# Layer two's attention steps in another order, and three pairs of banks in the last nested product: one Trainium2 core

## The chip, the core and the metric

The kernel runs on one core of a Trainium2 chip, in one launch. The core has five engines with a queue of instructions each, worked off strictly in order: TensorE (PE in the profile, with its weight loads as PEld), VectorE (DVE), ScalarE (ACT), GpSimd (POOL) and SyncE (SP, which here only issues DMA transfers). An engine goes on until an instruction needs something that another engine or a transfer hasn't finished; then everything behind it in that queue waits too. Matmuls write to PSUM, which has eight banks of 128 x 512 numbers. The metric is the device time of one execution in microseconds.

## What is computed

Two layers of linear attention and two of a gated mixer alternate on a sequence of 2048 rows of 512 numbers, all in fp32:

```python
def _A_ref(x, wqkv, wo):                    # H = 32, Dh = 16
    q, k, v = split_heads(x @ wqkv)
    phi = lambda t: jnp.where(t > 0, t + 1, jnp.exp(t)) + 1e-6
    pq, pk = phi(q), phi(k)
    kv = jnp.einsum("bhsd,bhse->bhde", pk, v)
    z = jnp.einsum("bhsd->bhd", pk)
    num = jnp.einsum("bhqd,bhde->bhqe", pq, kv)
    den = jnp.einsum("bhqd,bhd->bhq", pq, z)[..., None] + 1e-6
    return merge_heads(num / den) @ wo

def _B_ref(x, w_in, w_sp, b_sp, w_out):     # Fh = 896
    z = _gelu(jnp.einsum("bsd,df->bsf", x, w_in))
    z1, z2 = z[..., :Fh], _layernorm(z[..., Fh:], axis=-1)
    g = jnp.einsum("ts,bsf->btf", w_sp, z2) + b_sp[None, :, None]
    return jnp.einsum("bsf,fd->bsd", z1 * g, w_out)

x = A_x
x = x + _A_ref(_layernorm(x, axis=-1), A_wqkv, A_wo)
x = x + _B_ref(_layernorm(x, axis=-1), B_w_in, B_w_sp, B_b_sp, B_w_out)
x = x + _A_ref(_layernorm(x, axis=-1), A_wqkv, A_wo)
x = x + _B_ref(_layernorm(x, axis=-1), B_w_in, B_w_sp, B_b_sp, B_w_out)
```

## The kernel before

**Precision.** Each fp32 operand of a matmul is cut into a high part, which ScalarE rounds (`high`, line 132), and a low part, the rest, which VectorE subtracts (`low`, line 135). A product is then three matmuls (`mm3`, lines 146 to 148): high by high, high by low, low by high.

**Tiles.** Rows are worked on in 16 tiles of 128. In SBUF there are slots of several sizes: 22 pages ("pg", 128 x 512), 6 quads ("qd", four pages each), 4 larger ones ("bg") and the 16 tags z0 to z15. A slot is taken from the front of a list and put back at its end, and the next holder's first write waits for the last one's reads. The order of all instructions is the order in which the Python code issues them; nothing is rescheduled behind it.

**The attention loop (class `P1`, method `run`).** One step s works on several row tiles at once. `T_high(s)` transposes tile s on VectorE (line 327, its source is a copy that was written to DRAM turned, loaded by `turn.load`) and rounds it on ScalarE; `T_low(s)` subtracts. `K(s-1)` and `Q(s-1)` are 12 matmuls each, and `Gmm(s-2)` another 12, onto four banks which hold G over the whole loop. `K_phi` and `Q_phi` apply phi: two activations (lines 414, 415) and a sum on VectorE that reads the PSUM bank (line 416). `xsplit(s-1)` cuts the row tile itself, `K_split(s-1)` cuts phi(K) (lines 427 and 428) and lets GpSimd add it to a running sum (`zacc`, line 433). The Q of the last six tiles (`DEFER`) is put off into the steps behind the loop, so steps 11 to 16 have K and G only.

In layer two the same loop carries other work. `own.staged()` makes one part per step of the kept sums of the mixer's weights for the product N4: VectorE takes the low part of the sum before, ScalarE the high part of the next, VectorE adds or subtracts for the one after (lines 1244 to 1254), and SP stores parts and fetches pieces. From step 5 on, one piece per step of the weights wo and win2 is cut into high and low (`side`), and the next is fetched. Step 1 normalises the last row tile (`norm`), step 2 sends it to DRAM (`send`), step 15 loads wv into the quads in which the kept sums' pages lay until then.

In the order of issue, a step of layer two before the change is: loads of x and of the turned tile; T_high; K; T_low; K_phi; Q; xsplit; K_split; staged; Q_phi; Gmm; the side piece; the next side fetch.

**The nested product N4 (class `P4`, `nested_mm`).** The mixer's product w_sp by z2 is cut into block products; N1, N2 and N4 are themselves cut into seven (P1 to P7, Strassen in Winograd's form), each of two steps of 12 matmuls. Some of the seven add onto the banks of one before them. In N4, the last in layer two, VectorE adds or subtracts each of the seven, as soon as it is done, from the output (line 1468), and the banks go on being added to:

```python
NEST = {p: ("P1", "P2", "P6", "P5", "P7", "P3", "P4") for p in ("N1", "N2")}
NEST["N4"] = "P1", "P6", "P2", "P5", "P7", "P4", "P3"
```

with X (two banks) for P1, P6, P7, P4, and Y (two) for P2, and anew for P5 and P3. Step g issues, in this order: `prepare(g + 2, g + 3)` (high and low of weights, lines 1361 and 1370, and of the other operand), the matmuls, the sums if a product is done, `fetch(g + 4)`, gates on GpSimd (line 1548) and a load for the next gate. P1, P2 and P4 load 512 KB of raw weights per step on SP's queue (line 1314) and split them. P5, P6, P7 and P3 load 1024 KB per step on GpSimd's queue (line 1307): the kept sums, already split.

The functions that the change touches, with what calls them:

Of the kernel before, what the change touches and what calls it, by code (L numbers as in the profile page):

```python
# [11 lines left out]
F32R = mybir.dt.float32r  # L12
# [3 lines left out]
P = 128  # L16
# [10 lines left out]
DEFER = 6  # L27
# [57 lines left out]
def mixer_kernel(ctx: ExitStack, tc: tile.TileContext, x_in, wqkv, wo_d, win1_d, win2_d, wsp_d, bsp_d, wout_d,  # L85
# [246 lines left out]
    class P1:  # L332
# [91 lines left out]
        def K_split(self, i):  # L424
            r = self.r.pop(i)
            h, l = pages.get(PAGE, F32R), pages.get(PAGE, F32R)
            nc.scalar.activation(h, r, AF.Copy, bias=PHI_EPS)
            nc.vector.scalar_tensor_tensor(l, r, PHI_EPS, h.bitcast(F32), op0=OP.add, op1=OP.subtract)
            self.pk[i] = (h, l)
            if i == 0:  # L430
                self.zacc = r
            else:
                nc.gpsimd.tensor_tensor(r, self.zacc, r, op=OP.add)
                pages.put(self.zacc)
                self.zacc = r
# [22 lines left out]
        def xsplit(self, i):  # L458
            h, l = pages.get(PAGE, F32R), pages.get(PAGE, F32R)
            x = self.x.pop(i)  # L460
            if self.turn.turned(i):
                split(feats(h, False), feats(l, False), feats(x, True))
            else:
                split(h, l, x)
            pages.put(x)
            self.xhl[i] = (h, l)
# [80 lines left out]
        def run(self):  # L547
            side = deque()
            for w in (self.wo, self.win2):
                side.extend([w] * len(w.pieces))  # L550
            ND = NT - DEFER
            own = inner["N4"] if self.L == 1 else None
            if own is not None:
                spare = quads.get([P, 2, 2, 512]), quads.get([P, 2, 2, 512])
                own.home = Views(pages, *spare)
            else:
                self.wv = quads.get([P, 4, 512])
            each = 2 if own is None else 1
            for s in range(1, NT + 2):
                if s == 2 and own is not None:  # L560
                    self.send(NT - 1)
                self.loadx(s + 3 if own is None else s + 1)
# [22 lines left out]
                if own is not None and s <= NT:  # L585
                    own.staged()
                    if s == 1:
                        self.norm(NT - 1)
                    if s == NT - 1:
                        own.home.close()  # L590
                        own.home = pages
                        quads.put(*spare)
                        self.wv = quads.get([P, 4, 512])
# [9 lines left out]
                for c in (range(4) if s == NT - 1 else ()) if own is not None else range(s - 1, min(s, 4)):  # L603
                    nc.sync.dma_start(self.wv[:, c, :], wqkv[c * P:(c + 1) * P, 1024:1536])
                if s > 4:
                    for _ in range(min(len(side), 1 if s < 6 else each)):
                        side.popleft().piece()
                if s >= 4:
                    for w in list(side)[:1 if s < 5 else each]:
                        w.fetch()  # L610

# [655 lines left out]
    class P4:  # L1267
# [9 lines left out]
        NEST["N4"] = "P1", "P6", "P2", "P5", "P7", "P4", "P3"  # L1277
# [158 lines left out]
        def nested_mm(self, g):  # L1436
# [25 lines left out]
            if p == "N4":  # L1462
                for n, out in {"P1": ((1, self.X),), "P6": ((2, self.X),), "P2": ((1, self.Y),), "P5": ((4, self.Y),),
                               "P7": ((4, self.X),), "P3": ((2, self.Y),), "P4": ((3, self.X),)}[name]:
                    for i in range(2):
                        f = i if n % 2 else 2 + i
                        u = self.unit(n // 3, f)
                        (V.tensor_add if f == 3 else V.tensor_sub)(u, u, out[i])  # L1468
                if name in ("P2", "P3"):
                    banks.put(*self.Y)  # L1470
                elif name == "P4":
                    banks.put(*self.X)
                if name == "P3":
                    self.ready.extend((n, f, False) for n in range(2) for f in range(NF))
                return
            for i in range(2):
# [7 lines left out]
                elif name == "P2":  # L1484
                    V.tensor_add(u[1], u[1], self.Y[i])
# [8 lines left out]
                if name in ("P2", "P3"):  # L1494
                    banks.put(self.Y[i])
                elif name == "P4":
                    banks.put(self.X[i])
# [340 lines left out]
```

## Time and profile before

| | |
|---|---|
| three runs, median (lowest to highest) | 1377.22 us (1373.12 to 1379.17) |
| the profiled execution | 1374.07 us, of which the span is 1372.4 us |
| granted TensorE clock over the span | 0.999 |
| HBM traffic | 223 GB/s over the span |
| layer two's attention loop, steps 1 to 17 | from 691 to about 815 us of the span |
| N4, 14 steps | from 1251 to 1292 us of the span |

How to read what is quoted. A row of groups or of the timeline gives start and length in us (or a sum and a mean), the engine, the line of the code, the operation, and out<-in by the tiles' names; behind it in brackets stands how long the engine stood idle before it, and what ended that. The list of waits says which engine waited at which line, for which engine and line; then the sum in us, how often, and the longest. A row of the table of windows gives a stretch of the span, its length, the busy time of TensorE, its weight loads, VectorE, ScalarE and GpSimd with the number of instructions in brackets, the granted TensorE clock, the busy share of the DMA engines and GB/s. Matmuls overlap at their ends, so busy times of TensorE say little of its pace; starts and counts say more. A row of DMA issues gives the queue, how many, their size and the median us from issue to landing. The chain of waits is followed back from the last instruction of the span.

### The profile page before, as it was taken

How to read it: one execution, taken by the hardware profiler on the slowest of the kernel's cores; microseconds unless marked ns; L12 is line 12 of the kernel's file. 1: busy time of each engine (PE TensorE's matmuls, PEld its weight loads, DVE VectorE, ACT ScalarE, POOL GpSimd, SP SyncE). 2: the span in 40 equal slices, each digit the busy share in tenths (PEclk: the TensorE clock that was granted, in tenths of full speed). 3: DMA queues.
4: the chain of work that ended last, by engine and by line, in shares of the span. 5: the costliest groups of instructions: out<-in, count | busy, mean ns of one | idle time of the engine just before them, and what ended most of it. 6: DMA issues, size and time to landing. Idle time of an engine off the chain costs nothing. (4 is left out here: it accounts for less than half of the span.)

```text
span 1372.4 us, 18248 instructions
## 1 busy us (share of the span) xinstructions
PE 1359.8 (99%) x6105; PEld 1135.9 (83%) x6105; DVE 1024.9 (75%) x1541; ACT 627.2 (46%) x1004; POOL 468.9 (34%) x539
## 2 busy tenths in 40 slices
PE   9999999999999999999999999999999999999998
PEld 7888888888888888888888778888888888888787
DVE  6775888764747789988778868876767798878542
ACT  6775543444442442533456555544465534533310
POOL 3333475433334137427411233542230011313250
PEclk9999999999999999999999999999999999999999
DMA  5542477877778988888976533665568798568552
GB/s 171 177 131 62 121 239 252 265 256 269 249 258 288 312 275 277 272 324 286 319 215 187 174 108 115 207 207 192 193 207 281 223 339 316 198 199 298 211 184 90
DMA packets 182622, 306.95 MB, mean 224 GB/s; under 512 B 15488, under 2 KB 67584, under 8 KB 178432
## 3 DMA queue, kind: packets, MB, share of 16 engines
q1 hardware_dynamic: 174320, 265.81, 59.4%
q0 software_dynamic: 6336, 36.70, 7.4%
q10 hardware_dynamic: 1872, 3.28, 0.7%
q8 instruction: 48, 0.79, 0.3%
q14 instruction: 46, 0.38, 0.1%
HBM read 208.47 MB, written 97.26 MB: 223 GB/s over the span
## 5 line engine op out<-in xcount | busy, mean ns | idle before, releaser
L1526 PE MATMUL bank<-qd,pg 128*128 128x512 f32 x544 | 211.6, 389 | 0.0
L1527 PE MATMUL bank<-qd,pg 128*128 128x512 f32 x544 | 211.6, 389 | 0.0
L1528 PE MATMUL bank<-qd,pg 128*128 128x512 f32 x544 | 211.6, 389 | 0.0
L1370 DVE TENSOR_TENSOR qd<-qd,qd 128x1024 fp32r<-128x1024 f32 x104 | 147.2, 1416 | 68.2 <-ACT qd L1361 67.9
L1361 ACT ACTIVATE qd<-qd 128x1024 fp32r<-128x1024 f32 x104 | 110.1, 1058 | 125.0 <-DVE qd L1370 48.6
L132 ACT ACTIVATE pg<-pg 128x512 fp32r<-128x512 f32 (+1 forms) x154 | 94.9, 620 | 152.8 <-DVE pg L327 60.8
L148 PE MATMUL bank<-qd,pg 128*128 128x512 f32 x380 | 149.7, 394 | 0.2 <-DVE pg L135 0.2
L1117 POOL TENSOR_TENSOR pg<-pg,pg 128x512 f32<-128x512 f32 x64 | 92.7, 1449 | 138.6 <-DMA pg<-in_wsp_dram 84.4
L265 POOL TENSOR_SCALAR rs<-mv 128x1 f32<-128x1 f32 x95 | 46.9, 493 | 262.6 <-DVE mv L263 253.7
L276 ACT ACTIVATE pg<-pg,nb,rs 128x512 f32<-128x512 f32 x63 | 51.2, 813 | 170.6 <-POOL nb L270 170.3
L1548 POOL TENSOR_TENSOR bg<-bg,pg 128x512 f32<-128x512 f32 x56 | 90.8, 1631 | 110.4 <-DMA pg<-z 93.1
L135 DVE TENSOR_TENSOR pg<-pg,pg 128x512 fp32r<-128x512 f32 (+1 forms) x151 | 110.5, 733 | 18.7 <-ACT pg L132 11.2
L1527 PEld LDWEIGHTS bank<-qd,pg 128*128 128x128 f32 x544 | 102.1, 188 | 21.4
L1526 PEld LDWEIGHTS bank<-qd,pg 128*128 128x128 f32 x544 | 102.1, 188 | 21.2
L1528 PEld LDWEIGHTS bank<-qd,pg 128*128 128x128 f32 x544 | 102.1, 188 | 21.0
L146 PE MATMUL bank<-qd,pg 128*128 128x512 f32 x284 | 110.6, 390 | 0.0
L147 PE MATMUL bank<-qd,pg 128*128 128x512 f32 x284 | 110.6, 389 | 0.0
L327 DVE STREAM_TRANSPOSE pg<-pg 128x512 f32<-128x512 f32 x79 | 85.4, 1081 | 13.2 <-DMA z<-pg 4.9
L146 PE MATMUL bank<-bg,qd 128*128 128x448 f32 x256 | 94.1, 367 | 0.0
L147 PE MATMUL bank<-bg,qd 128*128 128x448 f32 x256 | 93.6, 366 | 0.0
L148 PE MATMUL bank<-bg,qd 128*128 128x448 f32 x256 | 93.5, 365 | 0.0
L1452 PE MATMUL bank<-qd,pg 128*128 128x512 f32 x224 | 87.3, 390 | 2.7 <-DVE bg L1468 2.6
(214 smaller groups left out, 3189.4 us busy)
## 6 DMA issues: line engine op xcount, KB each, us to landing
qd<-s SPq DMA_DIRECT2D x64, 512.0 KB, 4.0
qd<-n POOLq DMA_DIRECT2D x32, 1024.0 KB, 8.2
pg<-in_wsp_dram SPq DMA_DIRECT2D x103, 256.0 KB, 4.7
qd<-in_wsp_dram SPq DMA_DIRECT2D x40, 512.0 KB, 4.3
n<-pg SPq DMA_DIRECT2D x70, 256.0 KB, 4.4
s<-pg SPq DMA_DIRECT2D x64, 256.0 KB, 4.4
pg<-z SPq DMA_DIRECT2D x56, 256.0 KB, 4.2
x<-pg SPq DMA_DIRECT2D x48, 256.0 KB, 3.0
```

The costliest lines, as they stand in the source:

```text
L132: nc.scalar.activation(h, src, AF.Copy)
L135: nc.vector.tensor_sub(l, src, h.bitcast(F32))
L146: nc.tensor.matmul(out, ah, bh, start=start, stop=False)
L147: nc.tensor.matmul(out, ah, bl, start=False, stop=False)
L148: nc.tensor.matmul(out, al, bh, start=False, stop=stop)
L1117: nc.gpsimd.tensor_tensor(t, a, b, op=OP.add)
L1361: nc.scalar.activation(wh, r, AF.Copy)
L1370: nc.vector.tensor_sub(wl, r, wh.bitcast(F32))
L1526: m(out, h[:, o], w[:, 0, j, :], start=start, stop=False, skip_group_check=True)
L1527: m(out, h[:, o], w[:, 1, j, :], start=False, stop=False, skip_group_check=True)
L1528: m(out, l[:, o], w[:, 0, j, :], start=False, stop=stop, skip_group_check=True)
L1548: nc.gpsimd.tensor_tensor(u, u, z1, op=OP.mult)
```

## The change

`run` is parted into `first` (layer one) and `second` (layer two). `first` issues what `run` issued for layer one. `second` issues, per step: loads of the turned tile and of x (step 2's `send` behind them); **x_high**; T_high; K; **x_low**; T_low; **staged**; K_phi; Q; **the side piece's high**; K_high; **the side piece's low**; K_low; Q_phi; Gmm; the next side fetch; and in step 15 the four loads of wv as the last. `xsplit` and `K_split` are cut in two for that.

In N4 the seven products come in the order P1, P5, P6, P2, P7, P3, P4. P2 gets a pair of banks of its own, Z (in N1 and N2 too); Y is for P5 and P3, X for P1, P6, P7 and P4. The gates of the first two chunks of rows become ready behind P4 and no more behind P3, both being the last.

```diff
         def K_split(self, i):
+            self.K_high(i)
+            self.K_low(i)
+
+        def K_high(self, i):
+            self.pk[i] = h, l = pages.get(PAGE, F32R), pages.get(PAGE, F32R)
+            nc.scalar.activation(h, self.r[i], AF.Copy, bias=PHI_EPS)
+
+        def K_low(self, i):
             r = self.r.pop(i)
-            h, l = pages.get(PAGE, F32R), pages.get(PAGE, F32R)
-            nc.scalar.activation(h, r, AF.Copy, bias=PHI_EPS)
+            h, l = self.pk[i]
             nc.vector.scalar_tensor_tensor(l, r, PHI_EPS, h.bitcast(F32), op0=OP.add, op1=OP.subtract)
-            self.pk[i] = (h, l)
...
         def xsplit(self, i):
-            h, l = pages.get(PAGE, F32R), pages.get(PAGE, F32R)
+            self.x_high(i)
+            self.x_low(i)
+
+        def x_high(self, i):
+            self.xhl[i] = h, l = pages.get(PAGE, F32R), pages.get(PAGE, F32R)
+            t = self.turn.turned(i)
+            high(feats(h, False) if t else h, feats(self.x[i], True) if t else self.x[i])
+
+        def x_low(self, i):
+            h, l = self.xhl[i]
             x = self.x.pop(i)
             if self.turn.turned(i):
-                split(feats(h, False), feats(l, False), feats(x, True))
+                low(feats(l, False), feats(x, True), feats(h, False))
             else:
-                split(h, l, x)
+                low(l, x, h)
             pages.put(x)
...
+        def second(self, side):
+            ND = NT - DEFER
+            own = inner["N4"]
+            spare = quads.get([P, 2, 2, 512]), quads.get([P, 2, 2, 512])
+            own.home = Views(pages, *spare)
+            for s in range(1, NT + 2):
+                self.turn.load(s + 1)
+                self.loadx(s + 1)
+                if s == 2:
+                    self.send(NT - 1)
+                if s <= NT:
+                    self.x_high(s - 1)
+                if 2 <= s < NT:
+                    self.T_high(s)
+                if s == 1:
+                    self.K(0)
+                    self.K(1)
+                elif 2 < s <= NT:
+                    self.K(s - 1)
+                if s <= NT:
+                    self.x_low(s - 1)
+                if 2 <= s < NT:
+                    self.T_low(s)
+                if s <= NT:
+                    own.staged()
+                    self.K_phi(s - 1)
+                if s <= ND:
+                    self.Q(s - 1)
+                if s == NT + 1:
+                    self.late()
+                if s <= NT:
+                    lows = deque()
+                    if s > 4 and side:
+                        side.popleft().piece(lows=lows)
+                    self.K_high(s - 1)
+                    for l, src, h, r in lows:
+                        low(l, src, h)
+                        pages.put(r)
+                    self.K_low(s - 1)
+                if s == 1:
+                    self.norm(NT - 1)
+                if s <= ND:
+                    self.Q_phi(s - 1)
+                if s >= 2:
+                    self.Gmm(s - 2)
+                if s == NT + 1:
+                    self.late_phi()
+                if s >= 4 and side:
+                    side[0].fetch()
+                if s == NT - 1:
+                    own.home.close()
+                    own.home = pages
+                    quads.put(*spare)
+                    self.wv = quads.get([P, 4, 512])
+                    for c in range(4):
+                        nc.sync.dma_start(self.wv[:, c, :], wqkv[c * P:(c + 1) * P, 1024:1536])
...
-        NEST["N4"] = "P1", "P6", "P2", "P5", "P7", "P4", "P3"
+        NEST["N4"] = "P1", "P5", "P6", "P2", "P7", "P3", "P4"
...
                 if name == "P1":
                     self.X = [banks.get(PAGE) for _ in range(2)]
-                elif name in ("P2", "P5"):
+                elif name == "P2":
+                    self.Z = [banks.get(PAGE) for _ in range(2)]
+                elif name == "P5":
                     self.Y = [banks.get(PAGE) for _ in range(2)]
-            out = self.Y if name in ("P2", "P5", "P3") else self.X
+            out = self.Z if name == "P2" else self.Y if name in ("P5", "P3") else self.X
...
             if p == "N4":
-                for n, out in {"P1": ((1, self.X),), "P6": ((2, self.X),), "P2": ((1, self.Y),), "P5": ((4, self.Y),),
-                               "P7": ((4, self.X),), "P3": ((2, self.Y),), "P4": ((3, self.X),)}[name]:
-                    for i in range(2):
-                        f = i if n % 2 else 2 + i
-                        u = self.unit(n // 3, f)
-                        (V.tensor_add if f == 3 else V.tensor_sub)(u, u, out[i])
-                if name in ("P2", "P3"):
-                    banks.put(*self.Y)
-                elif name == "P4":
-                    banks.put(*self.X)
-                if name == "P3":
+                n = {"P1": 1, "P6": 2, "P2": 1, "P5": 4, "P7": 4, "P3": 2, "P4": 3}[name]
+                for i in range(2):
+                    f = i if n % 2 else 2 + i
+                    u = self.unit(n // 3, f)
+                    (V.tensor_add if f == 3 else V.tensor_sub)(u, u, out[i])
+                if name in ("P2", "P3", "P4"):
+                    banks.put(*out)
+                if name == "P4":
                     self.ready.extend((n, f, False) for n in range(2) for f in range(NF))
```

More of the change, by code (lines that the diff above doesn't have):

```diff
@@ L550, in run, with first @@
                 side.extend([w] * len(w.pieces))
-            ND = NT - DEFER
[L552 to L558, printed above, removed]
+            if self.L == 0:
+                self.first(side)
+            else:
+                self.second(side)
+        def first(self, side):
+            ND = NT - DEFER
+            self.wv = quads.get([P, 4, 512])
             for s in range(1, NT + 2):
-                if s == 2 and own is not None:
-                    self.send(NT - 1)
-                self.loadx(s + 3 if own is None else s + 1)
+                self.loadx(s + 3)
                 self.turn.load(s + 1)
@@ L584, in run @@
                     self.K_split(s - 1)
[L585 to L593, printed above, removed]
                 if s + 1 < NT and s + 1 in self.turn.by_pe:
@@ L602, in run @@
                     self.late_phi()
-                for c in (range(4) if s == NT - 1 else ()) if own is not None else range(s - 1, min(s, 4)):
+                if s <= 4:
+                    c = s - 1
                     nc.sync.dma_start(self.wv[:, c, :], wqkv[c * P:(c + 1) * P, 1024:1536])
-                if s > 4:
-                    for _ in range(min(len(side), 1 if s < 6 else each)):
+                else:
+                    for _ in range(min(len(side), 1 if s < 6 else 2)):
                         side.popleft().piece()
@@ L1484, in nested_mm @@
                 elif name == "P2":
-                    V.tensor_add(u[1], u[1], self.Y[i])
+                    V.tensor_add(u[1], u[1], out[i])
                 elif name == "P5":
@@ L1493, in nested_mm @@
                     V.tensor_add(u[3], self.X[i], bs[3])
[L1494 to L1497, printed above, removed]
+                if name in ("P2", "P3", "P4"):
+                    banks.put(out[i])
             if name == "P4" and p == "N2":
```

4 lines of the change are left out of this document (2 added, 2 removed).

## The prediction

> **What bounds the kernel now.** I read the busy line of the page first, then TensorE's waits, then the table of windows around them.
>
> ```profile
> span 1372.4 us, 18248 instructions
> PE 1359.8 (99%) x6105; PEld 1135.9 (83%) x6105; DVE 1024.9 (75%) x1541; ACT 627.2 (46%) x1004; POOL 468.9 (34%) x539
> ```
>
> ```profile
> PE bank L146 <- ACT z_h L132: 3.2, 2, 2.0
> PE bank L1452 <- DVE bg L1468: 2.6, 1, 2.6
> PE bank L496 <- DVE pg L491: 2.4, 1, 2.4
> ```
>
> ```profile
> 690.00:774.00 84.00, 84.00 (x372) 69.57 (x371) 69.30 (x89) 52.36 (x91) 15.74 (x12) 1.00 0.66 198
> 774.00:800.00 26.00, 22.80 (x88) 16.65 (x87) 20.95 (x27) 13.68 (x25) 4.85 (x3) 0.93 0.54 163
> 1099.00:1175.00 76.00, 75.92 (x335) 62.54 (x334) 69.02 (x122) 32.90 (x57) 8.22 (x16) 1.00 0.87 313
> 1250.00:1274.00 24.00, 24.00 (x108) 19.87 (x107) 21.23 (x31) 6.68 (x11) 11.90 (x11) 1.00 0.94 346
> 1274.00:1284.00 10.00, 7.32 (x32) 5.46 (x31) 6.35 (x11) 6.18 (x10) 0.53 (x1) 1.00 1.05 402
> ```
>
> TensorE sets the time: 99% busy, and the change neither adds nor removes a matmul. So only its gaps can be won, and the wait list names all that matter: two waits for a row split of layer two's attention (L146), one for N4's sums (L1452), and the start (L496), which isn't touched. Busy time hides slow matmuls, so I count instead. In the undisturbed window 690 to 774, 372 matmuls took 84.00 us: 0.2258 us each. From 774 to 800 there are 88, worth 88 x 0.2258 = 19.87 us, in 26.00: **6.13 us lost**. From 1274 to 1284, 32 x 0.2258 = 7.23 in 10.00: **2.77 us lost**. Together 8.9 us is about all that these two edits can win: 0.65% of 1377.22.
>
> **Attention: why TensorE waits.** Here are TensorE around the first wait and VectorE around it, in order of time.
>
> ```profile
> 775.03 0.39 PE L148 MATMUL bank<-pg,pg 128*128 128x512 f32 x1
> 777.45 0.50 PE L146 MATMUL bank<-qd,z_h 128*128 128x512 f32 x1 [2.04 <-ACT z_h L132]
> ...
> 779.20 0.63 PE L147 MATMUL bank<-qd,z_h 128*128 128x512 f32 x1
> 779.62 0.63 PE L148 MATMUL bank<-qd,pg 128*128 128x512 f32 x1
> ...
> 782.05 0.40 PE L146 MATMUL bank<-pg,pg 128*128 128x512 f32 x1
> ```
>
> ```profile
> 699.09 0.69 DVE L1250 TENSOR_TENSOR pg<-pg,pg 128x512 f32<-128x512 f32 x1
> ...
> 767.23 1.08 DVE L327 STREAM_TRANSPOSE pg<-pg 128x512 f32<-128x512 f32 x1
> 769.01 0.69 DVE L135 TENSOR_TENSOR pg<-pg,z_h 128x512 fp32r<-128x512 f32 x1 [0.70 <-ACT z_h L132]
> 770.16 0.69 DVE L416 SCALAR_TENSOR_TENSOR pg<-bank,pg 128x512 f32<-128x512 f32 x1 [0.46 <-ACT pg L415]
> ...
> 771.55 0.69 DVE L428 SCALAR_TENSOR_TENSOR pg<-pg,pg 128x512 fp32r<-128x512 f32 x1
> ...
> 772.76 1.79 DVE L1254 TENSOR_TENSOR qd<-qd 128x512 f32<-128x512 f32 x1
> 774.47 0.68 DVE L416 SCALAR_TENSOR_TENSOR z_q<-bank,z_q 128x512 f32<-128x512 f32 x1
> 775.07 0.68 DVE L135 TENSOR_TENSOR bg<-pg,bg 128x512 fp32r<-128x512 f32 x1
> 775.67 1.07 DVE L327 STREAM_TRANSPOSE pg<-pg 128x512 f32<-128x512 f32 x1
> ...
> 782.88 1.09 DVE L327 STREAM_TRANSPOSE pg<-pg 128x512 f32<-128x512 f32 x1
> ...
> 790.13 1.07 DVE L327 STREAM_TRANSPOSE pg<-pg 128x512 f32<-128x512 f32 x1
> ...
> 795.72 1.08 DVE L327 STREAM_TRANSPOSE pg<-pg 128x512 f32<-128x512 f32 x1
> ```
>
> ```profile
> 772.38 1.62 POOL L433 TENSOR_TENSOR pg<-pg,pg 128x512 f32<-128x512 f32 x1 [6.82 <-DMA n<-qd]
> ...
> 795.34 1.62 POOL L433 TENSOR_TENSOR pg<-pg,pg 128x512 f32<-128x512 f32 x1 [5.69 <-DVE pg L428]
> ```
>
> One round of the loop runs from one transpose (L327) to the next. VectorE's round is 775.67 - 767.23 = 8.44 us. TensorE's round is K, Q and G, 36 matmuls, 36 x 0.2258 = 8.13, so VectorE falls 0.3 us behind per round; from step 11 on there is no Q, TensorE needs 24 x 0.2258 = 5.42, and VectorE's rounds last 7.21 and 7.25. That is the debt which TensorE pays at 777.45 and again at 791.9.
>
> Of VectorE's 8.44 us, 0.70 and 0.46 are waits for ScalarE (the high half, the exponential), and the kept-sum add took 1.79 us against 0.69 for the same add at 699.09: it was issued while POOL's running sum (L433) ran from 772.38 to 774.00. The change puts the row split's subtraction into the 0.70 gap, puts the kept sum ahead of the K exponential's result (the 0.46 gap), and by that takes it out from behind L433.
>
> **What it costs.** No instruction is added: K_split, xsplit and the side pieces are cut into high and low, with the same activations and subtractions. The new round of VectorE, by durations: transpose 1.07, then three subtractions (x, T, kept low), the kept add, the K sum, the side low, K's low and the Q sum, 8 x 0.69 = 5.52: 6.6 us against TensorE's 8.13. From step 11 on without Q's sum and the kept add: 6.6 - 2 x 0.69 = 5.2 against 5.42.
>
> The new order has a collision of its own. L433 starts some 0.2 us after K's low and lasts 1.62; behind it VectorE now has Q's sum (one operand from PSUM) or the transpose, and then x's low, with two SBUF operands. The transpose at 795.72 ran inside the L433 of 795.34 and took its usual 1.08, so it pays nothing. x's low from step 11 on comes about 1.2 us after K's low and may wait 0.2 + 1.62 - 1.2 = 0.6, at most 1.79 - 0.69 = 1.1 as L1254 did; a late round of VectorE is then 5.2 + 0.6 = 5.8 to 5.2 + 1.1 = 6.3 us, above 5.42 (rival B). The Trainium skill's page "SBUF — State Buffer" (Who interferes with whom) has a rule against the change here: a VectorE instruction with two SBUF inputs is shut out for as long as a GpSimd instruction that reads SBUF holds the port they share. By that rule, the trace agrees: L1254 ended only 0.55 us after L433.
>
> Does the chain still arrive in time? ScalarE's part of it:
>
> ```profile
> 776.77 0.63 ACT L132 ACTIVATE z_h<-pg 128x512 fp32r<-128x512 f32 x1 [3.06 <-DVE pg L327]
> 777.31 0.58 ACT L414 ACTIVATE pg<-bank 128x512 f32<-128x512 f32 x1
> 777.92 0.63 ACT L415 ACTIVATE pg<-pg 128x512 f32<-128x512 f32 x1
> ```
>
> From the end of one K: two activations 1.21, K sum 0.69, K high 0.63, K low 0.69, transpose 1.07, x low 0.69, T low 0.69: 5.7 us, with seven handovers of about 0.1 some 6.4, with the collision 7.0 to 7.5. TensorE in that time has G, the next K and another G, 8.13 us, before it needs this T. It fits with 0.6 to 1.7 us to spare. So I take all but 0.2 of the 6.13: **-5.9 us**. Bounds: -6.3 (some small slow starts go too) and -2.3 (B).
>
> A part of that sum is the clock. K's 12 matmuls from 777.45 to 782.05 took 4.60 us where 2.71 are usual: 1.9 us, at 0.42 us each (779.20 to 779.62). The page "TensorE: Matmul & The Clock Gate" of the Trainium skill (What's actually happening) has the clock halve after about 3.4 us of idling, in a window that doesn't start with the kernel; by that rule a gap of 2.4 us, as here, would cost no clock. The measurement decides: it did. By the rule alone the win would be 1.9 smaller.
>
> SP's queue: the loads of x and of its turned copy now stand ahead of step 2's store, the stores of kept sums come earlier in the round, wv's four loads come behind the last side fetch. Nothing on TensorE waits for any of these within a round; I cost them at nothing, below at 0, above in rival C. The page-taking moves too: x's split takes two pages at the head of the round.
>
> **N4.** The chain of waits, then VectorE and TensorE at the stall:
>
> ```profile
> 1265.20 10.52 DMA qd<-in_wsp_dram
> 1275.82 1.07 ACT qd L1361
> ```
>
> ```profile
> 1279.33 1.22 DVE L1370 TENSOR_TENSOR qd<-qd,qd 128x1024 fp32r<-128x1024 f32 x1
> 1280.46 1.28 DVE L1468 TENSOR_TENSOR bg<-bg,bank 128x512 f32<-128x512 f32 x2
> ```
>
> ```profile
> 1278.34 0.39 PE L1455 MATMUL bank<-qd,pg 128*128 128x512 f32 x1
> 1281.29 0.47 PE L1452 MATMUL bank<-qd,pg 128*128 128x512 f32 x1 [2.56 <-DVE bg L1468]
> ```
>
> P4 adds onto X, which P7 has just left, so its first matmul waits for L1468 to read X; L1468 stood on VectorE behind the weight split L1370, whose load was 10.52 us under way. In the new order X, Y and Z take turns: after P7 come P3's 24 matmuls, 5.42 us, on Y. The stall without its usual 0.23 is 1281.29 - 1278.34 - 0.23 = 2.72. L1468 would have to be over 5.4 us late, and here it was 2.6. The matmuls, the sums (still two L1468 per product) and the weight splits stay as many and as long. Z costs two banks while P2 runs; X and Y hold four of the eight.
>
> What is late next is the data:
>
> ```profile
> qd<-n POOLq DMA_DIRECT2D x32, 1024.0 KB, 8.2
> ...
> qd<-in_wsp_dram SPq DMA_DIRECT2D x40, 512.0 KB, 4.3
> ...
> pg<-xt SPq DMA_DIRECT2D x45, 256.0 KB, 3.3
> ```
>
> The DMA engines are full here (0.94, 1.05). The kept sums come in loads of 1024 KB on POOL's queue, and go to TensorE without a split, and steps 2 to 5 now take four of them in a row where before there were two and two of 512 KB. That is 1 MB that must come earlier, 1024 KB at 346 GB/s = 3.0 us of DMA time. Against it, a slot comes free four steps ahead, 48 x 0.2258 = 10.8 us, over the 8.2 of such a load, and N1 and N2 have eight such loads in a row: from 1099 to 1175 335 matmuls took 76.00, where 75.64 are usual, 0.4 us lost in 76. Bounds: 0 and 3.0; I take 0.1, near N1 and N2. **-2.6 us**.
>
> **Sum.** 5.9 + 2.6 = 8.5. The profiled execution took 1374.07 (span 1372.4 and 1.7 around it): 1365.6. The runs shown, 1373.12, 1377.22 and 1379.17, put the median 3.15 above it. If that spread is loads coming late into N4, the change takes it away; if not, it stays. No row tells; I carry a third, 1.0: **1366.5**.
>
> **Rivals.**
> A. N4 stays DMA-bound: the four loads come late by their 3.0 us and the stall only changes its name. For it: the share of 1.05. Against: N1 and N2. Then 1374.07 - 5.9 + 0.3 + 1.0 = 1369.5.
> B. The port collision makes late rounds 6.3 us: 0.9 over 5.42 for six rounds is 5.4, less the spare 1.6: 3.8 of the 6.1 stay. For it: L1254's 1.79. Against: the chain starts anew from each K. 1374.07 - 2.3 - 2.6 + 1.0 = 1370.2.
> C. Slower. x's split holds two of the 22 pages half a round longer, and if with that the turned row's load has to wait for the page that the last G frees, the chain is load 3.3, transpose 1.07, high 0.63, low 0.69 = 5.7 behind G, where only the next K, 2.71, covers it: 3.0 us per round from step 11 to 16, 18 us in place of 6.1. 1374.07 + 11.9 - 2.6 + 1.0 = 1384.4. It decides from the point at which SP's load starts later than the G before it ends. Against: counted in the code, at the end of round 14 the pages held are x 2, turned row 1, T's lows 5, splits 4, running sum 1, side load 1, so 14 of 22.
> D. It doesn't do what it says: VectorE's queue is in order, and if x's low waits for ScalarE as long as T's low did, and N4's X for late weights, nothing moves: 1374.1 to 1377.2.
>
> **Chances.** Forecast 0.67, A 0.10, B 0.10, C 0.08, D 0.05. The forecast's own range is 1364 to 1369: 1365.6 with the spread carried in full (3.15) at the top, and at the bottom with that of the fastest run shown, 1373.12, 0.95 under the profiled one, and the lower bounds. A and B with the spread in full reach to 1372.4; C and D are left out, and 1.5 us are given below for gaps that I haven't listed: 1362.5 to 1372.5. What can be told from no change is 0.5%, 6.9 us, so faster means under 1370.3. Forecast mostly (0.57 of 0.67, since a baseline at its low end would halve the margin), half of A and a few of B: 0.64 faster; the rest of these and D 0.27 same; C and strays 0.09 slower.
>
> **What would show it.** Right: from 774 to 800 TensorE counts about 115 matmuls at clock 1.00; L1250 and its like take 0.69; no wait of L1452 on L1468. B: L135 at 1.3 to 1.8 behind each L433, with TensorE waiting on z_h at steps 13 to 16. A: TensorE waiting on the DMA of qd<-n in N4's steps 4, 5, 8 or 9. C: L327 waiting on xt's load. The prediction fails if TensorE's gaps move to a third place, or if the median's extra 3 us is no part of the profiled execution's gaps.

## The result, and the profile after

| | before | after |
|---|---|---|
| median of the runs (lowest to highest) | 1375.73 us (1373.12 to 1379.17, 4 runs) | 1365.39 us (1364.2 to 1365.68, 4 runs) |
| profiled execution, and its span | 1374.07, 1372.4 us | 1364.2, 1362.2 us |
| lost by TensorE from 774 to 800 us, counted | 6.1 us | 0 |
| lost by TensorE in N4, counted | 2.8 us | 0 |

The ratio is 0.9922, with a 95% interval from 0.9897 to 0.9947. Faster by 0.8%, as forecast; the time lies 1.1 us under the 1366.5 predicted, and the runs lie much closer together.

The counts come out a little low, because a window counts each matmul that only touches its edges, one or two too many. Added up from one start of a matmul to the next, with the usual 0.227 us taken off, TensorE lost 6.4 us from 774 to 800 and 3.2 us in N4 in the kernel before, and nothing in either after. The span fell by 10.2 us: these 9.6, less 0.4 that are lost anew (below), and some 0.9 more in two places that the change doesn't touch, the first 20 us and a start near 1020 us. Both scatter: the first 20 us lose between 2.7 and 3.6 us in the traces of these kernels.

What TensorE waits for after the change:

```profile
PE bank L510 <- DVE pg L505: 2.4, 1, 2.4
PE bank L148 <- DVE pg L135: 0.2, 1, 0.2
PE bank L541 <- ACT pg L132: 0.2, 1, 0.2
```

The 2.4 us at the start (L510, L496 before) remain, and two waits of 0.2, one near the start (L541) and one behind the attention loop (L148, at 844.5 us). Both waits for z_h and the one for L1468 are gone. The table of windows (length, busy time and count of TensorE, its weight loads, VectorE, ScalarE, GpSimd; clock, DMA share, GB/s):

```profile
690.00:774.00 84.00, 84.00 (x370) 69.06 (x370) 63.72 (x95) 55.80 (x96) 13.85 (x12) 1.00 0.64 209
774.00:800.00 26.00, 26.00 (x117) 21.52 (x116) 21.21 (x29) 15.68 (x28) 6.65 (x5) 1.00 0.43 148
1240.00:1264.00 24.00, 24.00 (x108) 19.87 (x107) 21.66 (x29) 8.77 (x18) 12.17 (x13) 1.00 1.00 367
```

Two readings. From 774 to 800 TensorE now counts 117 matmuls where there were 88, and the clock stays at 1.00: all of the 6.1 us is back. From 690 to 774 it counts 370 where there were 372: 2 x 0.2258 = 0.45 us have been lost in a new place, in front of the old one. And in N4 the DMA engines are as full as before (1.00 over these 24 us), without a wait of TensorE.

VectorE and GpSimd around steps 10 to 12 of the loop, after the change:

```profile
764.03 0.69 DVE L1315 TENSOR_TENSOR qd<-qd 128x512 f32<-128x512 f32 x1
766.00 0.69 DVE L416 SCALAR_TENSOR_TENSOR pg<-bank,pg 128x512 f32<-128x512 f32 x1 [1.28 <-ACT pg L415]
...
769.20 1.07 DVE L327 STREAM_TRANSPOSE pg<-pg 128x512 f32<-128x512 f32 x1
770.13 0.66 DVE L135 TENSOR_TENSOR pg<-pg,pg 128x512 fp32r<-128x512 f32 x1
...
776.09 1.09 DVE L327 STREAM_TRANSPOSE pg<-pg 128x512 f32<-128x512 f32 x1
777.04 1.05 DVE L135 TENSOR_TENSOR pg<-pg,pg 128x512 fp32r<-128x512 f32 x1
...
781.60 1.09 DVE L327 STREAM_TRANSPOSE pg<-pg 128x512 f32<-128x512 f32 x1
782.54 1.13 DVE L135 TENSOR_TENSOR pg<-pg,pg 128x512 fp32r<-128x512 f32 x1
```

```profile
768.23 1.30 POOL L439 TENSOR_TENSOR pg<-pg,pg 128x512 f32<-128x512 f32 x1 [6.95 <-DVE pg L435]
776.25 1.29 POOL L439 TENSOR_TENSOR pg<-pg,pg 128x512 f32<-128x512 f32 x1 [6.72 <-DVE pg L435]
```

The kept add (L1315) takes 0.69 us, and VectorE stands idle for 1.28 before K's sum. It waits for ScalarE's exponential (L415), and ScalarE had waited for K's matmuls: VectorE waits for TensorE now, no more TensorE for it. The new collision is there as forecast: from step 11 on x's low behind the transpose takes 1.05 and 1.13 us in place of 0.66, while GpSimd's running sum (L439) runs. It costs 0.4 to 0.5 us in these rounds, and TensorE doesn't feel it.

### The profile page after: what moved, and what is told of

Its sections match the earlier page's. It is cut to its first block, busy times and chain, and to the rows that moved or that the text cites. A ratio compares the mean times of both kernels' runs of the same rounds, so it can differ in the third digit from the quotient of the medians.

```text
span 1362.2 us, 18282 instructions
## 1 busy us (share of the span) xinstructions
PE 1355.5 (100%) x6105; PEld 1135.3 (83%) x6105; DVE 1007.3 (74%) x1541; ACT 628.5 (46%) x1004; POOL 465.9 (34%) x539
## 4 chain that ended last, share of the span: by engine, by line
PE 97%; DVE 2%; ACT 1%; issue 0%; POOL 0%; DVEq 0%; ACTq 0%; POOLq 0%
PE bank L148 19%; PE bank L146 19%; PE bank L147 19%; PE bank L1585 9%; PE bank L1584 9%; PE bank L1586 9%; PE bank L1517 4%; PE bank L1518 4%; PE bank L1515 4%; PE bank L969 1%; PE bank L968 1%; PE bank L967 1%; PE bank L708 1%; PE bank L288 0%; DVE pg L135 0%
## 5 line engine op out<-in xcount | busy, mean ns | idle before, releaser
L1431 DVE TENSOR_TENSOR qd<-qd,qd 128x1024 fp32r<-128x1024 f32 x104 | 143.9, 1383 | 69.9 <-ACT qd L1422 69.6
L148 PE MATMUL bank<-qd,pg 128*128 128x512 f32 x380 | 148.5, 391 | 0.2 <-DVE pg L135 0.2
L1178 POOL TENSOR_TENSOR pg<-pg,pg 128x512 f32<-128x512 f32 x64 | 95.6, 1493 | 136.4 <-DMA pg<-in_wsp_dram 88.2
L148 PE MATMUL bank<-bg,qd 128*128 128x448 f32 x256 | 93.4, 365 | 0.0
```

The source lines that it names most:

```text
L148: nc.tensor.matmul(out, al, bh, start=False, stop=stop)
L1178: nc.gpsimd.tensor_tensor(t, a, b, op=OP.add)
L1431: nc.vector.tensor_sub(wl, r, wh.bitcast(F32))
```

## The experiments

### Each half alone

e1: class `P1` as changed, class `P4` as before. e2: the reverse.

> Layer two's attention steps in the new order, N4 as before. Theory (two causes that add up): nothing is lost from 774 to 800 us, TensorE's wait for z_h is gone, and N4 keeps its wait of L1452 on L1468 of 2 to 3 us: the span is 1372.4 - 6.2 = 1366.2 (1365.5 to 1367). If the 6 us of scatter between runs of the kernel before came from N4's late loads, it stays here; if it came from the attention stalls, it is gone (under 2 us). Rival (one cause: N4's stall hangs on the phase of its loads, and that on what happened before): with 6 us won earlier, N4's stall goes as well, and the span is 1363 or less.

> N4 in the new order with three pairs of banks, attention as before. Theory: no wait in N4, the attention stalls stay with some 6.1 us: the span is 1372.4 - 3.0 = 1369.4 (1369 to 1370). Scatter: the other half of what the attention-only kernel tells. Rival (the four loads of 1024 KB in a row are only in time because TensorE came earlier or later): a wait on qd<-n of 1 us or more appears in N4.

| kernel | median (lowest to highest) | ratio to the kernel before, interval | span |
|---|---|---|---|
| before, same chip | 1373.61 us (1372.93 to 1375.72, 15 runs) | | |
| attention only | 1368.8 us (1367.21 to 1371.99, 5 runs) | 0.996 (0.9946 to 0.9973) | 1369.7 |
| N4 only | 1371.29 us (1370.46 to 1372.07, 11 runs) | 0.9981 (0.9972 to 0.999) | 1368.7 |

Windows of the attention-only kernel, then of the N4-only kernel; 26 us hold 115 matmuls and 20 us hold 88.6 at full pace, and one or two more are counted at the edges:

```profile
774.00:800.00 26.00, 26.00 (x116) 21.54 (x115) 21.19 (x29) 16.56 (x29) 5.67 (x5) 1.00 0.48 159
1264.00:1284.00 20.00, 16.84 (x67) 13.14 (x66) 11.24 (x18) 8.29 (x14) 5.40 (x6) 0.91 0.83 314
```

```profile
774.00:800.00 26.00, 22.75 (x88) 16.67 (x87) 21.00 (x27) 13.59 (x24) 4.95 (x4) 0.93 0.55 161
1264.00:1284.00 20.00, 20.00 (x90) 16.57 (x89) 17.46 (x23) 10.88 (x17) 7.78 (x8) 1.00 0.95 351
```

Each half takes away its own loss and leaves the other's. In this execution of the attention-only kernel N4 lost 20 - 67 x 0.2258 = 4.9 us, where 2.8 had been lost before, of it a part at the lower clock (0.91), and the span came to 1369.7 and not to 1366.2. But it is the longest of five. The other four have spans of 1364.9, 1366.0, 1366.5 and 1367.9 us, so the median, 1366.5, lies within the range that was expected (1365.5 to 1367). The medians of the times are 4.8 us (attention) and 2.3 us (N4) under the kernel before, 7.1 together; e8 below, the changed kernel but for its first step, wins 9.7 on the same chip. So the halves seem to be worth somewhat more together than one by one. The rival that N4's stall hangs on what came before may have a point, with the other sign: where the attention is fast, the stall doesn't vanish, it grows. How much of that a usual run has isn't known. The scatter sides with N4: five runs of the attention-only kernel lie 4.8 us apart and fifteen of the kernel before 2.8, all with the old N4, and eleven with the new one 1.6, although the attention stalls are in all of these eleven.

### N4: order or banks

e3 swaps the last two products only:

```diff
-        NEST["N4"] = "P1", "P6", "P2", "P5", "P7", "P4", "P3"
+        NEST["N4"] = "P1", "P6", "P2", "P5", "P7", "P3", "P4"
...
-                if name == "P3":
+                if name == "P4":
                     self.ready.extend((n, f, False) for n in range(2) for f in range(NF))
```

e4 keeps the old order and issues the splits behind the sums:

```diff
+                late = p == "N4" and k >= 8
+                if not late:
+                    self.prepare(g + 2, g + 3)
-                self.prepare(g + 2, g + 3)
...
                 self.mm(g)
+                if late:
+                    self.prepare(g + 2, g + 3)
```

> The kernel before, only the last two products of N4 change places (P1, P6, P2, P5, P7, P3, P4), two pairs of banks as before. Theory (the stall is P4 adding onto the bank that P7 has just left): the stall of 2.7 goes fully, N4 loses under 0.4 us, the span is 1369.4 to 1369.8. Rival (it takes the alternation throughout, since P6 also follows P1 on X, and P7's loads come in another order): 1 us or more stays in N4.

> The kernel before, order of N4 as before; from its ninth step on the weight split and the other operand's split are issued behind the step's matmuls and sums, no more ahead of them. Theory (VectorE's queue: L1468 stood behind L1370): the stall falls from 2.7 to 0.6 to 1.2, what it takes to read the first X bank after P7's last matmul on it, and L1370 may be what comes next. Rival (the late load sets it whatever the queue's order): the stall stays at 2.5 or more.

TensorE's waits in N4, of e3 and then of e4:

```profile
PE bank L1452 <- DMA qd<-n: 0.6, 2, 0.3
```

```profile
PE bank L1452 <- DMA qd<-n: 1.5, 1, 1.5
```

The wait of L1452 on L1468 is gone in both, also in e4, where the order of the products and the banks are the old ones. So it was what the prediction said: the sums stood behind the weight splits in VectorE's queue. For e4, 0.6 to 1.2 us of it were expected to stay, and nothing did. VectorE in e4 shows what that expectation overlooked:

```profile
1278.36 0.69 DVE L1468 TENSOR_TENSOR bg<-bg,bank 128x512 f32<-128x512 f32 x1 [1.88 <-PE bank L1455]
```

```profile
1276.71 0.47 PE L1452 MATMUL bank<-qd,pg 128*128 128x512 f32 x1 [1.48 <-DMA qd<-n]
...
1279.29 0.39 PE L1455 MATMUL bank<-qd,pg 128*128 128x512 f32 x1
1279.52 0.39 PE L1452 MATMUL bank<-qd,pg 128*128 128x512 f32 x1
```

The sums come bank by bank. P7 is through with the first X bank six matmuls before its end, and with nothing ahead of it in the queue L1468 reads that bank from 1278.36 to 1279.05, while P7 still writes the other; P4's first matmul follows at 1279.52 without a gap. What is late in its place is the data: one step earlier TensorE stood 1.48 us for a load of kept sums. In e3, too, the loads come next, and there its window is short by more than its two listed waits of 0.3:

```profile
1264.00:1284.00 20.00, 19.41 (x85) 15.44 (x84) 13.82 (x23) 6.53 (x12) 6.12 (x7) 1.00 1.04 390
```

85 matmuls are worth 19.2 us of 20, so 0.8 are lost, 1.1 from start to start. The theory of e3 (under 0.4) fell short; its rival (1 us or more), which had named P7's loads beside the banks, fits. e3 and e4 are single runs, 1371.9 and 1372.18 us, with spans of 1370.2 and 1370.5. The N4-only kernel's runs reach from 1370.46 to 1372.07, so the times don't tell the three apart; the waits do. In e3's order six loads of kept sums come in a row (P5, P7, P3), in the full new order never more than four (P5 and P6, then P7 and P3), and with these TensorE waits for none in N4. But the old order, which e4 has, also has no more than four in a row, so the reason why they come in time in the new one is not shown.

### The attention loop: one move at a time

e5 moves the kept sums' part only; e6 moves the row split only; e7 leaves the order as it was and takes GpSimd's running sum away in layer two; e9 is the changed kernel with the kept sums' part back behind K's low.

```diff
 # e5
+                if own is not None and s <= NT:
+                    own.staged()
                 if s <= NT:
                     self.K_phi(s - 1)
...
                 if own is not None and s <= NT:
-                    own.staged()
 # e6
+                if own is not None and s <= NT:
+                    self.x_high(s - 1)
                 if turned:
                     self.T_high(s)
...
+                if own is not None and s <= NT:
+                    self.x_low(s - 1)
                 if turned:
                     self.T_low(s)
...
-                    self.xsplit(s - 1)
+                    if own is None:
+                        self.xsplit(s - 1)
                     self.K_split(s - 1)
 # e7
             if i == 0:
                 self.zacc = r
+            elif self.L == 1:
+                pages.put(r)
             else:
 # e9
                 if s <= NT:
-                    own.staged()
                     self.K_phi(s - 1)
...
                     self.K_low(s - 1)
+                    own.staged()
```

> The kernel before, layer two: only the kept sums' part moves, from behind K's split to ahead of K's sum; the row split and the side pieces stay where they were. Theory (the debt is VectorE's round of 8.44 us against TensorE's 8.13, of which 1.1 is the wait behind the running sum and 0.46 a gap): the kept add takes 0.69, the round falls to about 7 us, and of the 6.4 us lost from 774 to 800 at most 0.5 stays. Rival (only all three moves together make the late rounds short enough): 2 us or more stays.

> The kernel before, layer two: only the row split moves, its high half ahead of the transpose and its low half into the 0.70 us gap. Theory: the kept add still takes 1.79 behind the running sum, the round is 8.44 - 0.7 = 7.7, so no debt by step 10, but steps 11 and 12 take some 6.5 us against 5.42: 0.3 to 1.5 us of the 6.4 stays. Rival (the wait behind the running sum is the cause, the gaps don't matter): 4 us or more stays.

> The kernel before, in its old order; in layer two GpSimd's running sum of phi(K) is left out, so that layer's normaliser counts the first row tile alone. Theory (the wait behind the running sum is 1.1 us of each round): the kept add takes 0.69 in place of 1.79, the round is 7.3 us, steps 11 and 12 some 6.1, and 0 to 1 us of the 6.4 stays. Rival (VectorE's gaps are the cause, not the shared port): the kept add keeps 1.79 or the loss stays at 4 us or more.

> The changed kernel, but the kept sums' part goes back behind K's low, where GpSimd's running sum holds it up; the row split and the side pieces stay moved. Theory A (any 0.4 us per round that VectorE saves is enough; with only the row split moved the gap merely went to K's low, here the side piece's low fills that): the kept add takes 1.79, the round is about 7.7 us and stays tied to TensorE's 8.16, and from 774 to 800 us at most 1.5 of the 6.4 us comes back. Theory B (only the place of the kept sums counts): 4 us or more comes back.

| kernel, one run each | time | span | lost by TensorE from 774 to 800 us |
|---|---|---|---|
| e5, kept sums first, old N4 | 1371.6 us | 1369.9 | 0 |
| e6, row split first, old N4 | 1373.76 us | 1372.1 | 26 - 88 x 0.2258 = 6.1 |
| e7, no running sum, old N4 | 1368.98 us | 1367.3 | 0 |
| e9, kept sums last, new N4 | 1365.29 us | 1363.2 | 0.2 (one matmul fewer than e5) |

The first three keep the old N4 with its own waits, so their spans don't tell of attention alone; the window does. From 774 to 800 us, e5, e6, e7 and e9 in this order:

```profile
774.00:800.00 26.00, 26.00 (x116) 21.53 (x115) 20.21 (x29) 16.20 (x29) 7.01 (x5) 1.00 0.55 170
```

```profile
774.00:800.00 26.00, 22.78 (x88) 16.73 (x87) 20.69 (x28) 13.38 (x25) 4.80 (x3) 0.93 0.54 162
```

```profile
774.00:800.00 26.00, 26.00 (x116) 21.55 (x115) 20.26 (x30) 16.48 (x29) 0.00 (x0) 1.00 0.54 176
```

```profile
774.00:800.00 26.00, 26.00 (x115) 21.15 (x114) 21.51 (x31) 17.31 (x31) 5.88 (x4) 1.00 0.55 170
```

Moving the kept sums alone wins everything, and so does taking the running sum away in the old order. Moving the row split alone wins nothing; a third wait of TensorE, 0.7 us, even follows behind the window, at 804 us. VectorE in e6, one round:

```profile
758.59 1.08 DVE L327 STREAM_TRANSPOSE pg<-pg 128x512 f32<-128x512 f32 x1
759.53 0.67 DVE L135 TENSOR_TENSOR pg<-pg,pg 128x512 fp32r<-128x512 f32 x1
760.44 0.69 DVE L135 TENSOR_TENSOR pg<-pg,pg 128x512 fp32r<-128x512 f32 x1 [0.24 <-ACT pg L132]
...
762.98 0.69 DVE L428 SCALAR_TENSOR_TENSOR pg<-pg,pg 128x512 fp32r<-128x512 f32 x1 [0.70 <-ACT pg L427]
...
764.19 1.79 DVE L1263 TENSOR_TENSOR qd<-qd,qd 128x512 f32<-128x512 f32 x1
...
767.11 1.07 DVE L327 STREAM_TRANSPOSE pg<-pg 128x512 f32<-128x512 f32 x1
```

The 0.70 us gap behind the transpose shrank to 0.24, and a new one of 0.70 opened ahead of K's low (L428), which waits for K's high half: in the old order x's low had covered exactly that. The round is 767.11 - 758.59 = 8.52 us, no shorter than the 8.44 before. My theory of e6, 7.7 us, was wrong for that reason; its rival's 4 us or more stayed.

VectorE in e7, where nothing of GpSimd's runs:

```profile
769.03 0.69 DVE L1256 TENSOR_TENSOR qd<-qd 128x512 f32<-128x512 f32 x1
```

And in e9, where the kept sums are back behind the running sum, but the side piece's low stands in the gap ahead of K's low:

```profile
756.96 1.07 DVE L327 STREAM_TRANSPOSE pg<-pg 128x512 f32<-128x512 f32 x1
...
760.50 0.68 DVE L135 TENSOR_TENSOR bg<-pg,bg 128x512 fp32r<-128x512 f32 x1
761.28 0.69 DVE L435 SCALAR_TENSOR_TENSOR pg<-pg,pg 128x512 fp32r<-128x512 f32 x1
...
762.49 1.78 DVE L1311 TENSOR_TENSOR qd<-qd,qd 128x512 f32<-128x512 f32 x1
...
764.80 1.07 DVE L327 STREAM_TRANSPOSE pg<-pg 128x512 f32<-128x512 f32 x1
```

The kept add still takes 1.78, yet the round is 764.80 - 756.96 = 7.84 us, under TensorE's 8.13, and only some 0.2 of the 6.4 us are lost again. Theory A holds in what it says of the loss. So there are two sufficient ways out, and the change takes both: either the kept add out of the running sum's way (1.1 us per round), or both other moves together (8.44 - 7.84 = 0.6). The side pieces' move by itself was not run.

### The new loss, and the smallest edit

e8: in the changed kernel, `K_phi(0)` of step 1 ahead of `staged()`.

```diff
+                if s == 1:
+                    self.K_phi(0)
                 if s <= NT:
                     own.staged()
+                if 1 < s <= NT:
                     self.K_phi(s - 1)
```

e10: e5's class `P1`, the changed class `P4`. e11: the changed kernel again, beside e10.

> The changed kernel, but in step 1 alone K's phi comes ahead of the kept sums' part. Theory: the changed kernel's new loss of 0.4 us at 704 us comes from step 1, where ScalarE loads its table for the exponential (1.28 us) behind the kept part's high half, so that step 2's transpose is late; with phi first it goes, and the span is 1361.8 against 1362.2, which the times of the runs can't tell. Rival (step 2's late x or turned load): the 0.4 stays.

> The smallest edit that the runs so far point to: the kernel before, with only the kept sums' part ahead of K's sum in layer two, and the new N4. Theory: nothing lost in N4 nor from 774 to 800, the 0.4 us at 704 as in the changed kernel: span 1362 to 1363, and times within 1 us of the changed kernel beside it. Rival (the other two moves carry a part): 1 us or more slower than the changed kernel.

> The changed kernel as it is, on the same chip as the two before it, for comparison: 1364 to 1366 us, runs within 2 us of each other, the span 1362 to 1363.5, no wait of TensorE over 0.5 us behind the start.

| kernel | median (lowest to highest, 4 runs each) | ratio, interval | span |
|---|---|---|---|
| e8 | 1364.82 us (1364.48 to 1366.12) | 0.9928 (0.9909 to 0.9946) | 1362.3 |
| e10 | 1364.79 us (1364.13 to 1365.57) | 0.9919 (0.9899 to 0.9938) | 1363.2 |
| e11 | 1365.97 us (1364.94 to 1366.36) | 0.9926 (0.9903 to 0.9949) | 1363.7 |

(Before: 1374.53 us beside e8, 1376.44 beside the other two.) The window ahead of the old stall in e8:

```profile
690.00:774.00 84.00, 84.00 (x372) 69.60 (x371) 63.62 (x95) 56.49 (x96) 13.31 (x12) 1.00 0.64 211
```

It holds 372 matmuls again: the new loss came from step 1, where the kept sums' part went ahead of the first phi. The span didn't follow (1362.3 against 1362.2), so 0.4 us can't be told here. e10 does what the whole change does, by two of its four edits: its runs overlap those of the changed kernel, and the row split's and the side pieces' moves carry nothing that can be measured. Its median is 1.2 us lower than that of e11, where at most 1 us either way was expected, and the spans of e10 and e11 came out 0.2 above their ranges; in both, a load made one matmul of layer one start 0.4 us late, at 607 us. Of the 1.2 us, 0.3 lie outside the span: e10's times are 1.7 us longer than its spans, as in the kernel before, e11's 1.9 to 2.0. No run shows why. No version beat the changed kernel by more than the runs scatter.

## Why the prediction was right, step by step

**What bounds the kernel: right.** All that was lost in the two named places came back, and nothing else of the kernel had to change for it. But 8.9 us was not all that could be won there: by the starts it was 9.6.

**Attention, -5.9 us: right in size.** 6.4 us by the starts (6.1 counted) are gone from the window and 0.4 were lost anew at its front. The way there was half right. That the kept add waits for GpSimd's running sum was the cause; e7 shows it without moving a single instruction, and the rule of the Trainium skill's "SBUF — State Buffer" (Who interferes with whom) agrees: two SBUF inputs wait, and with GpSimd still the same add takes 0.69 us. The step that failed is "puts the row split's subtraction into the 0.70 gap": filling that gap alone gives nothing (e6), since the subtraction had been covering another wait. With the side piece in the second gap it would have been enough by itself (e9). I counted both as parts of one sum; they are two alternatives.

Where the loss comes from was misread too. I had VectorE fall 0.3 us behind in each round, 8.44 us against TensorE's 36 matmuls. ScalarE, then TensorE, in the kernel before, in that same round:

```profile
768.34 0.63 ACT L132 ACTIVATE z_h<-pg 128x512 fp32r<-128x512 f32 x1 [3.07 <-DVE pg L327]
```

```profile
769.82 0.39 PE L146 MATMUL bank<-qd,z_h 128*128 128x512 f32 x1
772.53 0.39 PE L146 MATMUL bank<-pg,pg 128*128 128x512 f32 x1
```

K from 769.82 and G from 772.53 are all that TensorE has ahead of the K that starts at 777.45: 24 matmuls, 5.4 us, and no Q. The 8.44 us already stood against a short round. The 0.3 us of the five rounds of 8.5 us before it had only used up VectorE's lead, which at 769.82 was down to 769.82 - 768.97 = 0.85 us. The loss came from the next three rounds: 8.44, 7.21 and 7.25 against 5.4 each are 6.6 us too much, 5.7 of them beyond the lead, nearly all of the 6.4. At the same K e5 has 6.2 us of lead, with rounds of 8.02, 6.77 and 5.59 us behind it, and e9 4.1 us, with 7.89, 5.59 and 5.62: in both the lead covers the excess. Both ways out do two things at once: they leave VectorE a lead, and they shorten the late rounds.

**The collision of x's low: right.** Forecast 0.6 and at most 1.1 us, measured 0.4 to 0.5; rival B needed it to hold TensorE up, and it didn't.

**The clock as a part of the sum: wrong.** I put 1.9 of the 6.13 us down to the halved clock. In e4 the attention loop is the old one, and the same window reads

```profile
774.00:800.00 26.00, 21.61 (x88) 15.38 (x87) 20.99 (x27) 13.63 (x25) 4.93 (x4) 1.00 0.55 161
```

at full clock throughout: the same 88 matmuls, the same 6.1 us lost. VectorE's late rounds set the loss; where the clock is lower, TensorE's slow matmuls only fill time that it would have spent waiting. Nothing came of this error, since the whole wait went.

**N4, -2.6 us: right.** 2.8 us as counted, 3.2 by the starts, are gone. VectorE and ScalarE at P4's weights after the change:

```profile
1274.09 1.23 DVE L1431 TENSOR_TENSOR qd<-qd,qd 128x1024 fp32r<-128x1024 f32 x1 [1.38 <-ACT qd L1422]
```

```profile
1273.00 1.06 ACT L1422 ACTIVATE qd<-qd 128x1024 fp32r<-128x1024 f32 x1 [8.40 <-DMA qd<-in_wsp_dram]
```

The raw weights are late still (ScalarE stood idle for 8.40 us until they landed), and their split ends at 1275.3, with P4 starting 1.3 us later, at 1276.66. Rival A wasn't far: with half measures (e3, e4) TensorE does wait for kept sums.

**The spread, 1.0 of 3.15 us carried: near, by a guess.** Runs with the new N4 lie 1.4 to 1.7 us apart (changed kernel, e2, e8, e10, e11), those of the kernel before 2.8 apart beside e1 and up to 6.4 (1373.21 to 1379.65 beside e10). That points to N4; no profile of the longer runs of the kernel before shows it. Of the 3.15 us, 1.2 are left between the profiled execution and the median, so the spread didn't make the 1.1 us between forecast and result. These come from the profiled execution itself, 1364.2 against 1365.6: its span fell by 10.2 us and not by 8.5. N4 gave 0.6 more than its term, attention 0.1, and 0.9 came in the two places outside the change, which is luck; the time outside the span took 0.3 back (2.0 us after, 1.7 before).

**C and D: not seen.** No wait of a transpose on its load held TensorE up.

What stays open: why N4's stall in the old order was larger when the attention was fixed. TensorE's waits in N4, for e1, e5 and e7, which have fast attention and the old N4:

```profile
PE bank L1513 <- DVE bg L1529: 3.1, 1, 3.1
```

```profile
PE bank L1453 <- DVE bg L1469: 3.5, 1, 3.5
...
PE bank L1453 <- DMA qd<-n: 1.4, 1, 1.4
```

```profile
PE bank L1454 <- DVE bg L1470: 2.0, 1, 2.0
...
PE bank L1454 <- DMA qd<-n: 0.4, 1, 0.4
```

These are single executions, e1's the longest of its five, and the old N4 scatters by itself; that the loads' phase does it was only argued.

## What to carry to other kernels

Where one engine is 99% busy, count its instructions per window against its undisturbed pace: that gave each loss to 0.4 us, while busy times and the list of waits show only a part; adding up the starts is closer still. Before a subtraction is moved into a gap, look at what it covers where it stands. Set each round of one engine against what the other has to do in that same round, and ask how much lead is left: here the rounds of 8.5 us against 8.13 cost only lead, and three rounds against 5.4 cost the time. And once the lead covers the excess, a second saving wins nothing, so parts of such a change can't be priced by leaving one out.

## What the runs showed of the hardware

The TensorE clock dropped in the attention stall of the kernel before, of e2, e3 and e6 (0.93 over the window) and not in e4 (1.00). The waits of e4 and then of e6 are of one length:

```profile
PE bank L146 <- ACT z_h L132: 4.4, 3, 2.1
```

```profile
PE bank L146 <- ACT z_h L132: 3.9, 3, 2.1
```

The longest was 2.1 us in both, 2.0 in the kernel before. The Trainium skill's "TensorE: Matmul & The Clock Gate" (What's actually happening) speaks of an idle window of about 3.4 us; here less was enough, in some executions and not in others.

The traces show what decides. Between the first matmuls and the last, a stretch at half clock lasts 3.41 us in all of the traces that have one, and the stretches at full clock between two such stretches are whole multiples of that: 590.51 us in the kernel before (173 times), 587.09 in e2 (172), 88.75 in e1 (26). Laid on this raster, from the first record of the clock on (5 to 9 us into the span), every stretch of 3.41 us in which TensorE stood idle for 1.97 us or more by the profile was followed by one at half clock, in all thirteen traces, and none in which it was 1.87 or less. In the kernel before the whole wait of 2.04 us lies in one of them, from 774.53 to 777.95 us, and the next is at half clock. In e4 the wait of 2.10 us is cut by an edge at 776.87, into 1.45 and 0.65.

GpSimd's running sum took 1.62 us in the kernel before, next to VectorE's kept add, and 1.30 and 1.29 in the changed kernel in the rows shown above. Of the ten from 740 to 805 us one was long again:

```profile
798.32 0.69 DVE L135 TENSOR_TENSOR pg<-pg,pg 128x512 fp32r<-128x512 f32 x1
...
798.54 1.61 POOL L439 TENSOR_TENSOR pg<-pg,pg 128x512 f32<-128x512 f32 x1 [3.55 <-DVE pg L435]
```

It started 0.22 us after x's low, a subtraction with two SBUF operands, and this time the sum is the one that took longer. That fits a port that holds up whichever of the two comes second. The other traces agree: in the twelve that have the running sum, each sum of layer two's loop that started while an instruction of VectorE with two SBUF operands was under way took 1.52 to 1.68 us, and each of the others 1.28 to 1.31. In the kernel before nearly all are of the first kind, so there the sum came second to a subtraction and the kept add second to the sum, and both took longer.
